# Rounding the split weights with one integer addition, and scoring two heads at once, in an attention and mixture-of-experts kernel

## The chip, the core and the metric

The program runs on one core of one Trainium2 chip. The core has TensorE (PE, matmuls and transposes), VectorE (DVE), ScalarE (ACT), GpSimd (POOL) and SyncE (SP, which here issues nearly all DMAs). Each engine executes its own queue in order and waits on semaphores for the others; a matmul writes a bank of PSUM, and every copy out of PSUM is DVE's or ACT's work. The metric is the device time of one execution, in microseconds.

## What is computed

Local attention with 32 global tokens for 4 batches of 8 heads, then a dense layer pair, then a layer in which each token goes to one of 8 experts. The arithmetic is float32; the dense weights arrive as 64-bit floats.

```python
def _attn_ref(q_l, k_l, v_l, q_g, k_g, v_g):      # (4, 8, 512 or 32, 64)
    s_g = scale * q_g @ concat(k_g, k_l).T;  out_g = softmax(s_g) @ concat(v_g, v_l)
    s_ll = scale * q_l @ k_l.T;  s_ll = where(|i - j| <= 32, s_ll, -1e9)
    s_l = concat([scale * q_l @ k_g.T, s_ll])
    out_l = softmax(s_l) @ concat(v_g, v_l)
    return concat([out_g, out_l])
def _moe_ref(x, w_in, w_out):                     # 2176 x 512, 512 x 2048, 2048 x 512
    h = x @ w_in
    return maximum(0.01 * h, h) @ w_out
def _moe2_ref(x, expert_emb, tau, w1, w2):        # 8 experts, 512 x 1024 and 1024 x 512
    logits = normalized(x) @ normalized(expert_emb).T / tau
    e = argmax(logits);  gate = softmax(logits)[e]
    return gate * (maximum(x @ w1[e], 0) @ w2[e])
```

## The kernel before

The work stands in one program order, which a scheduler turns into a queue for each engine. On PE the order is kept as written; on the other engines the scheduler chooses within the priorities given (`ahead` gives attention's parts a head start of 50).

**Attention** goes by pairs of heads, `n` = 0 to 15. `QK(n, 0)` transposes the keys and `QK(n, 1)` the queries, so that head 0 lies in partitions 0 to 63 and head 1 in 64 to 127. A unit `u` = 0 to 63 is two query blocks of 128 for one head: `S(u)` multiplies queries and keys (two matmuls of 128 rows by 224 keys), takes scores plus mask and the row minimum on DVE (line 213), the exponential with its row sum on ACT (218), adds 1e-9 and inverts the sum on DVE (222, 223), and scales block 0 on POOL and block 1 on DVE (229). For the first four head pairs the queries lie in a zero-padded tile and the matmul uses all 128 rows (line 201); later it uses the 64 rows of its head (203). The probabilities are in one of three buffers `prs`. `TR(u)` transposes them two slots later; ACT copies them out (240). `AV(p)` multiplies two units with the values, four slots after. `GS`, `GT` and `GA` do the global rows for two head pairs. `load_v` fetches the values; a second copy, shifted by 64 keys with the global values behind it (`vb`), is made by two ACT copies (116, 117).

**The dense weights** are 32 pieces of 128x512, each loaded as pairs of 32-bit words into one of two `raw` buffers. `conv_abs` takes the magnitude of the high words on ACT (357). `conv_bits` is five DVE steps: clamp (367), shift and mask (368), sign and exponent put in (371, which begins a second temporary), exponent alone (374), low word times 2^-52 times that (375). `conv_add` adds the two temporaries on POOL (384), `conv_split` rounds to the matmul's format on ACT (390) and subtracts for the remainder on POOL (391). Each `conv()` call finishes one piece, works on the next and loads ahead.

**The dense layers**: `L1(i, f)` is twelve matmuls (684) into an accumulator, then copy (ACT, 691), leaky step (DVE, 692), rounding (ACT, 694) and remainder (DVE, 695); `L2` is six matmuls (706 to 708) for two tiles of tokens, one step later. Up to slot 21 there is attention and conversion alone; then each of the first steps has one `L1`, one `L2`, one `conv()` and 0.65 slots of attention, until all pieces are converted; then the dense steps and attention go on, and the experts' layer follows (from about 660 us in the trace).

PSUM's eight banks are four pools of two, `S`, `H`, `Y` and `T`; the tables `ALONE`, `FUSED` and `MIXED` say in which pool a tile lies in each stretch (before: scores in `S`, `H`, `S`).

Of the kernel before, what the change touches and what calls it, by code (L numbers as in the profile page):

```python
# [18 lines left out]
P = 128  # L19
# [6 lines left out]
def kernel(  # L26
# [53 lines left out]
    NPAD = 4  # L80
# [24 lines left out]
    def load_v(n):  # L105
# [10 lines left out]
        nc.scalar.copy(vb[0:64], ve[0:64, 1:NC + 1])  # L116
        nc.scalar.copy(vb[64:96], ve[0:32, 0:1].to_broadcast([SG, NC, 2, D]))
# [22 lines left out]
    for t in [qz] + gzs:  # L140
        nc.vector.memset(t[D:P, 0], 0.0)
        nc.vector.memset(t[0:D, 1], 0.0)
# [7 lines left out]
    bank = {"sp": "S", "sg1": "S"}  # L150
# [6 lines left out]
    def QK(n, j):  # L157
        qn, kn, gn = natural[n]
        if j == 1:
# [4 lines left out]
            if n < NPAD:  # L164
                nc.scalar.copy(qz[0:D, 0], qv[0:D])
                nc.vector.tensor_copy(qz[D:P, 1], qv[D:P])
            else:
                nc.scalar.copy(qz[:, n % 2], qv)
# [24 lines left out]
    def S(u):  # L193
        n, c0, h = u // 4, 2 * ((u // 2) % 2), u % 2
        kT, _ = qkT[n]
        r = slice(D * h, D * h + D)
        sp = ps.tile([P, 2, WK], F32, tag=bank_of("sp"), name="sp")
        for i in range(2):
            c = c0 + i
            if n < NPAD:  # L200
                nc.tensor.matmul(sp[:, i, :], qz[:, h, c * P:(c + 1) * P], kT[:, c, :], start=True, stop=True)
            else:
# [4 lines left out]
        pr = prs[u % NPR]  # L207
        nm = att.tile([P, 2], F32, tag="nm", bufs=4, name="nm")
        sm = att.tile([P, 2], F32, tag="sm", bufs=4, name="sm")
        for i in range(2):  # L210
            c = c0 + i
            m = 0 if c == 0 else (2 if c == NC - 1 else 1)
            nc.vector.tensor_tensor_reduce(  # L213
                out=pr[:, i, 0:WK], in0=sp[:, i, :], in1=mask[:, m, :], scale=-0.125, scalar=BIG,
                op0=ALU.add, op1=ALU.min, accum_out=nm[:, i:i + 1],
            )
        for i in range(2):
            nc.scalar.activation(  # L218
                out=pr[:, i, 0:WK], in_=pr[:, i, 0:WK], func=AF.Exp, bias=nm[:, i:i + 1], scale=-1.0,
                accum_out=sm[:, i:i + 1],  # L220
# [3 lines left out]
        for i in range(2):  # L224
            eng = "pv"[i]
# [999 lines left out]
```

## Time and profile before

| | us |
|---|---|
| runs before | 965.29, 965.67, 968.04 (median 965.67) |
| the profiled execution | 967.12 |
| its span, first to last instruction | 965.4 |
| PE busy | 899.1 (93%) |
| DVE busy | 696.4 (72%) |
| ACT busy | 564.2 (58%) |
| POOL busy | 280.2 (29%) |

The profiler recorded one execution; all rows quoted come from it. Shares over the whole span mix three stages: attention with weight conversion, the dense layers with the rest of attention, and the experts. The stages have different late engines, so each is read in its own stretch. [...]

### The profile page before, as it was taken

The page shows a single profiled execution, that of the slowest core. Times are in us where ns is not written, and L with a number is a line of the kernel's source. Part 1 is how long each engine was busy: PE and PEld are TensorE (multiplying, and loading weights), DVE is VectorE, ACT ScalarE, POOL GpSimd, SP SyncE. Part 2 cuts the span into 40 slices and gives each one's busy share as a digit, 9 for nine tenths or more (in the row PEclk, how much of TensorE's full clock was granted, in tenths as well). Part 3 has the DMA queues.
Part 4 walks back from the last instruction along what each step waited for, and adds up shares of the span by engine and source line. Part 5 has one row for each costly group of instructions (what it writes and reads, how often), then busy time and mean ns, then how long its engine had stood idle before and what let it go on. Part 6 is the DMA issues. An engine that isn't in the chain of part 4 may idle for free.

```text
span 965.4 us, 16184 instructions
## 1 busy us (share of the span) xinstructions
PE 899.1 (93%) x5578; PEld 747.9 (77%) x5578; DVE 696.4 (72%) x1722; ACT 564.2 (58%) x1206; POOL 280.2 (29%) x316
## 2 busy tenths in 40 slices
PE   7688877979999999999999999997799999999997
PEld 5565766768888888887888888986687888888885
DVE  7999999997554554544553534564988999999996
ACT  6777545465545554454452323256477888888885
POOL 4767656663121121121110100020223321222211
PEclk9987988989999999999999999999799999999999
DMA  6843333341011011010000000254613416919650
GB/s 163 186 121 110 111 108 102 91 132 24 23 39 43 23 38 42 1 39 20 2 12 13 12 12 12 60 170 186 51 48 119 134 44 221 359 33 381 210 201 25
DMA packets 92454, 89.82 MB, mean 93 GB/s; under 512 B 61191, under 2 KB 69511, under 8 KB 92370
## 3 DMA queue, kind: packets, MB, share of 16 engines
q1 hardware_dynamic: 88146, 77.99, 26.6%
q0 software_dynamic: 4224, 10.78, 4.0%
q8 instruction: 45, 0.74, 0.4%
q14 instruction: 39, 0.32, 0.1%
HBM read 137.14 MB, written 11.63 MB: 154 GB/s over the span
## 4 chain that ended last, share of the span: by engine, by line
PE 62%; issue 5%; DVE 5%; DMA 3%; ACT 1%; POOL 0%; SPq 0%; POOLq 0%; DVEq 0%
PE hps L684 16%; PE hp L910 9%; PE yp L938 8%; PE yp L706 6%; PE yp L708 5%; PE yp L707 5%; PE sp L203 3%; PE av L252 2%; PE pp L238 1%; PE tp L924 1%; DVE w2s L865 1%; DVE w1s L865 1%; DMA ids<-idl 1%; PE lp L514 1%; DMA out_dram<-yo,ids 1%
## 5 line engine op out<-in xcount | busy, mean ns | idle before, releaser
L692 DVE SCALAR_TENSOR_TENSOR gf<-gf 128x256 f32<-128x256 f32 (+1 forms) x144 | 62.9, 445 | 121.0 <-ACT gf L691 120.7
L910 PE MATMUL hp<-w1s,xgT 128*128 128x512 f32 x528 | 139.0, 413 | 0.0
L691 ACT COPY gf<-hps 128x256 f32<-128x256 f32 (+1 forms) x144 | 50.1, 359 | 145.8 <-PE hps L684 143.3
L938 PE MATMUL yp<-w2s,ht 128*128 128x512 f32 x528 | 130.8, 396 | 1.0 <-DVEq L1189 1.0
L938 PEld LDWEIGHTS yp<-w2s,ht 128*128 128x128 f32 x528 | 98.8, 188 | 25.7 <-DVEq L1189 1.4
L706 PE MATMUL yp<-woh,g 128*128 128x512 f32 x272 | 115.4, 424 | 1.8 <-ACT g L694 1.8
L910 PEld LDWEIGHTS hp<-w1s,xgT 128*128 128x128 f32 x528 | 100.0, 196 | 21.2
L708 PE MATMUL yp<-woh,g 128*128 128x512 f32 x272 | 108.9, 400 | 4.3 <-DVE g L695 4.3
L229 POOL TENSOR_SCALAR pr<-pr,sm 128x224 f32<-128x224 f32 x64 | 65.4, 1021 | 160.5 <-DVE sm L223 130.3
L707 PE MATMUL yp<-wol,g 128*128 128x512 f32 x272 | 108.3, 398 | 0.0
L694 ACT CAST g<-gf 128x256 fp32r<-128x256 f32 (+1 forms) x144 | 55.3, 394 | 71.5 <-DVE gf L692 71.5
L695 DVE TENSOR_TENSOR g<-gf,g 128x256 fp32r<-128x256 f32 (+1 forms) x144 | 66.2, 468 | 31.2 <-ACT g L694 25.9
L684 PE MATMUL hps<-xs,wih 128*128 128x256 f32 x448 | 77.6, 296 | 11.0 <-DVE nm L213 11.0
L684 PEld LDWEIGHTS hps<-xs,wih 128*128 128x128 f32 x448 | 66.8, 195 | 18.4 <-DVE nm L213 12.3
L684 PE MATMUL hps<-xl,wih 128*128 128x256 f32 x448 | 72.9, 285 | 0.0
L684 PE MATMUL hps<-xs,wil 128*128 128x256 f32 x448 | 72.6, 285 | 0.0
L946 POOL DMA_INDIRECT out_dram<-yo,ids x22 | 26.2, 1191 | 157.0 <-ACT yo L945 150.2
L218 ACT ACTIVATE pr<-pr,nm 128x224 f32<-128x224 f32 x128 | 60.8, 477 | 18.2 <-DVE nm L213 17.9
L708 PEld LDWEIGHTS yp<-woh,g 128*128 128x128 f32 x272 | 51.6, 190 | 19.3 <-DVE g L695 7.1
L684 PEld LDWEIGHTS hps<-xs,wil 128*128 128x128 f32 x448 | 62.6, 194 | 0.0
L684 PEld LDWEIGHTS hps<-xl,wih 128*128 128x128 f32 x448 | 62.6, 194 | 0.0
L706 PEld LDWEIGHTS yp<-woh,g 128*128 128x128 f32 x272 | 51.4, 189 | 14.0 <-issue 4.6
(267 smaller groups left out, 1933.7 us busy)
## 6 DMA issues: line engine op xcount, KB each, us to landing
w1a<-in_moe_w_dram SPq DMA_DIRECT2D x12, 2048.0 KB
w2a<-in_moe_w_dram SPq DMA_DIRECT2D x12, 2048.0 KB
w1b<-in_moe_w_dram SPq DMA_DIRECT2D x12, 2048.0 KB
w2b<-in_moe_w_dram SPq DMA_DIRECT2D x12, 2048.0 KB
raw<-in_moe_w_in_dram SPq DMA_DIRECT2D x16, 512.0 KB
raw<-in_moe_w_out_dram SPq DMA_DIRECT2D x16, 512.0 KB
x2d<-x SPq DMA_DIRECT2D x16, 256.5 KB
kn<-in_k_l_dram SPq DMA_DIRECT2D x32, 128.0 KB
```

The lines of the kernel that those rows point to most:

```text
L218: nc.scalar.activation(out=pr[:, i, 0:WK], in_=pr[:, i, 0:WK], func=AF.Exp, bias=nm[:, i:i + 1], scale=-1.0, accum_out=sm[:, i:i + 1],)
L229: (nc.gpsimd if eng == "p" else nc.vector).tensor_scalar(out=pr[:, i, 0:WK], in0=pr[:, i, 0:WK], scalar1=sm[:, i:i + 1], scalar2=None, op0 ...
L684: nc.tensor.matmul(hps, ws[a][:, k], xs[c][k], start=(a + c + k == 0), stop=((a, c) == (1, 0) and k == KM - 1))
L691: nc.scalar.copy(gf, hps[:, cs])
L692: nc.vector.scalar_tensor_tensor(out=gf, in0=gf, scalar=0.01, in1=gf, op0=ALU.mult, op1=ALU.max)
L694: nc.scalar.copy(g[:, 0], gf)
L695: nc.vector.tensor_tensor(out=g[:, 1], in0=gf, in1=g[:, 0].bitcast(F32), op=ALU.subtract)
L706: nc.tensor.matmul(yp, g[:, 0], hi, start=(f == 0), stop=False)
L707: nc.tensor.matmul(yp, g[:, 0], lo, start=False, stop=False)
L708: nc.tensor.matmul(yp, g[:, 1], hi, start=False, stop=(f == KF - 1))
L910: nc.tensor.matmul(hp_, xT[:, a, k, :], w[:, c, k, :], start=(a + c + k == 0), stop=(c == 1 and k == KM - 1))
L938: nc.tensor.matmul(yp, ht[:, a, f, :], w[:, c, f, :], start=(j + a + c + f == 0), stop=(j == c == 1 and f == 3))
```

## The change

Three things change. **The weights**: ACT makes two passes over a raw piece, the magnitude of the high words and the low words times 2^-29 as integers; DVE does clamp, shift and mask, sign and exponent, and then one integer addition of the two, which carries the rounding into the upper bits. POOL's addition goes; all pieces now lie in one temporary from ACT's first pass to POOL's subtraction. **The scores**: one call does both heads of a query block pair, alternating between the two halves of PE's rows, into two banks; probabilities have four buffers, queries one unpadded one; the sums of two units are added to and inverted together, and the scaling is half DVE's and half ACT's instead of half POOL's. **The values**: the shifted copy is loaded by five DMAs per head pair instead of two ACT copies. The tables of banks follow.

```diff
-        nc.scalar.copy(vb[0:64], ve[0:64, 1:NC + 1])
-        nc.scalar.copy(vb[64:96], ve[0:32, 0:1].to_broadcast([SG, NC, 2, D]))
+        for h in range(2):
+            part = v_l[b, h0 + h, 96:96 + 3 * P].rearrange("(c p) d -> p c d", p=P)
+            nc.sync.dma_start(vb[0:64, 0:NC - 1, h, :], part[0:64])
+            nc.sync.dma_start(vb[64:96, :, h, :], v_g[b, h0 + h].unsqueeze(1).to_broadcast([SG, NC, D]))
+        nc.sync.dma_start(vb[0:32, NC - 1], v_l[b, hs, 480:512].rearrange("h s d -> s h d"))
...
-    NPR = 3
+    NPR = 4
-    qz = att.tile([P, 2, NC * P], F32, name="qz")
+    qz = att.tile([P, NC * P], F32, name="qz")
...
+        sps = [ps.tile([P, 2, WK], F32, tag=bank_of(f"sp{h}"), name="sp") for h in range(2)]
         for i in range(2):
             c = c0 + i
+            for h in range(2):
+                r = slice(D * h, D * h + D)
                 nc.tensor.matmul(
-                    sp[:, i, :], qz[r, n % 2, c * P:(c + 1) * P], kT[r, c, :], start=True, stop=True,
+                    sps[h][:, i, :], qz[r, c * P:(c + 1) * P], kT[r, c, :], start=True, stop=True,
                     tile_position=(D * h, 0),
                 )
...
-        for i in range(2):
-            eng = "pv"[i]
...
+        for j in range(4):
+            pr = pr2[j // 2][:, j % 2, 0:WK]
+            if j % 2:
+                nc.scalar.activation(out=pr, in_=pr, func=AF.Copy, scale=sm[:, j:j + 1])
             else:
+                nc.vector.tensor_scalar(out=pr, in0=pr, scalar1=sm[:, j:j + 1], scalar2=None, op0=ALU.mult)
...
+            nc.scalar.activation(out=pair[0].bitcast(F32), in_=raws[i][:, :, :, 1].bitcast(F32), func=AF.Abs)
+            nc.scalar.activation(out=pair[1], in_=raws[i][:, :, :, 0].bitcast(U32), func=AF.Copy, scale=2.0 ** -29)
...
-        nc.vector.tensor_scalar(out=t0, in0=t2, scalar1=-0x800000, scalar2=None, op0=ALU.bitwise_and)
-        nc.vector.scalar_tensor_tensor(
-            out=t0.bitcast(F32), in0=low.bitcast(U32), scalar=2.0 ** -52, in1=t0.bitcast(F32),
-            op0=ALU.mult, op1=ALU.mult,
-        )
-            nc.gpsimd.tensor_tensor(out=t2.bitcast(F32), in0=t2.bitcast(F32), in1=t0.bitcast(F32), op=ALU.add)
+        nc.vector.tensor_tensor(out=t, in0=t, in1=low, op=ALU.add)
...
-    ALONE = dict(sp="S", sg1="S", pp="H", av="Y", gp="Y", gq="T", ga="T", qp="T", kp="T", gnp="T")
-    FUSED = dict(sp="H", sg1="H", pp="H", av="T")
-    MIXED = dict(sp="S", sg1="S", pp="S", av="S", gp="T")
+    ALONE = dict(sp0="S", sp1="H", sg1="S", pp="Y", av="T", gp="Y", gq="T", ga="T", qp="T", kp="T", gnp="T")
+    FUSED = dict(sp0="H", sp1="T", sg1="H", pp="H", av="T")
+    MIXED = dict(sp0="S", sp1="T", sg1="S", pp="S", av="S", gp="T")
```

How the queues move is seen at three places. In the changed kernel's order the names are the same and the line numbers differ by a few.

On ACT, around the first copy of a dense accumulator (`gf<-hps`), before: `t` is a first pass over a raw piece, `wih` and `woh` the rounding, `pr` an exponential.

```order
L390 CAST woh<-t_989 128x512
L357 ACTIVATE t_1094<-raw 128x512
L218 ACTIVATE pr_99,sm<-pr_99,nm 128x224 x2
L261 COPY xr<-av 128x256
L240 COPY pT<-pp 128x512
L282 ACTIVATE pg,gm<-sg_1136,gm 128x512
L283 ACTIVATE pg,gm<-sg_1137,gm 128x32
L691 COPY gf<-hps 128x256
```

And now, where L359 and L360 are the two passes, L382 the rounding, L217 the exponentials and L226 the scalings:

```order
L382 CAST wih<-t_1221 128x4x128
L217 ACTIVATE pr_97,sm<-pr_97,nm 128x224 x2
L217 ACTIVATE pr_98,sm<-pr_98,nm 128x224 x2
L360 ACTIVATE t_1349<-raw 128x512
L259 COPY xr<-av 128x256
L238 COPY pT<-pp 128x512
L359 ACTIVATE t_1348<-raw 128x512
L382 CAST woh<-t_1278 128x512
L226 ACTIVATE pr_97<-pr_97,sm 128x224
L226 ACTIVATE pr_98<-pr_98,sm 128x224
L682 COPY gf<-hps 128x256
```

Exponentials of two units stand together and their scalings in the same queue behind them. Ahead of this first copy stand 10 passes over raw pieces and 8 roundings before, 30 and 14 now; 12 copies of values before, none now; 22 scalings now.

On DVE, one piece of the conversion among attention's work, before:

```order
L374 TENSOR_SCALAR t_872<-t_989 128x512
L223 RECIPROCAL sm<-sm 128x2
L213 ISA pr_98,nm<-sp,mask 128x224
L213 ISA nm 128x1
L213 ISA pr_98,nm<-sp,mask 128x224
L213 ISA nm 128x1
L375 SCALAR_TENSOR_TENSOR t_872<-raw,t_872 128x512
L229 TENSOR_SCALAR pr_99<-pr_99,sm 128x224
```

And now, from the third step (L372) and the integer addition (L375) on:

```order
L372 SCALAR_TENSOR_TENSOR t_1278<-raw,t_1278 128x512
L375 ISA t_1278<-t_1278,t_1279 128x1024
L221 TENSOR_SCALAR sm<-sm 128x4
L222 RECIPROCAL sm<-sm 128x4
L228 TENSOR_SCALAR pr_97<-pr_97,sm 128x224
L228 TENSOR_SCALAR pr_98<-pr_98,sm 128x224
L368 TENSOR_SCALAR t_1348<-t_1348 128x512
```

The addition is a special instruction that the order lists over 1024 elements, two 16-bit halves of each of the 512 words; the sums of two units (128x4) go through one add and one reciprocal.

On PE, one step of the dense layers with scores and AV in it, after the conversion has ended, before:

```order
L684 MATMUL hps<-xs,wil 128x256 x4
L203 MATMUL sp<-kT,qz 128x224 x2
L252 MATMUL av<-pT,ve_110 64x128 x2
L252 MATMUL av<-pT,vb_112 64x128 x2
L252 MATMUL av<-pT,ve_110 64x128 x2
L252 MATMUL av<-pT,vb_112 64x128 x2
L706 MATMUL yp<-woh,g 128x512
```

And now:

```order
L675 MATMUL hps<-xs,wil 128x256 x4
L200 MATMUL sp<-kT,qz 128x224 x4
L250 MATMUL av<-pT,ve_109 64x128 x2
L250 MATMUL av<-pT,vb_111 64x128 x2
L250 MATMUL av<-pT,ve_109 64x128 x2
L250 MATMUL av<-pT,vb_111 64x128 x2
L697 MATMUL yp<-woh,g 128x512
```

The four score matmuls of two units stand together where AV stands, and the odd slot that held two of them before holds none.

## Rows read from the trace of the kernel before

**Rows 1.** Busy us by stretch: PE, PEld, DVE, ACT, POOL; clock; DMA share; GB/s.

```profile
0.00:86.00 86.00, 66.49 (x502) 49.10 (x503) 77.13 (x275) 62.18 (x171) 53.26 (x83) 0.90 0.61 148
86.00:225.00 139.00, 114.38 (x764) 93.24 (x762) 136.30 (x292) 74.15 (x187) 86.77 (x75) 0.91 0.37 106
225.00:660.00 435.00, 432.31 (x2960) 373.50 (x2959) 217.08 (x838) 196.11 (x561) 67.48 (x95) 1.00 0.13 37
0.00:10.00 10.00, 4.55 (x15) 3.54 (x16) 5.17 (x25) 3.68 (x5) 4.28 (x27) 1.00 0.61 139
```

**Rows 2.** Groups of DVE, 0 to 225: count, busy us, mean ns, idle.

```profile
L375 DVE SCALAR_TENSOR_TENSOR t<-raw,t 128x512 f32<-128x512 uint32 x32 | 29.1, 911 | 0.3
...
L222 DVE TENSOR_SCALAR sm<-sm 128x2 f32<-128x2 f32 x35 | 12.2, 347 | 1.0 <-ACT pr L218 0.8
```

**Rows 3.** Lines of DVE, 0 to 225: shortest/median/longest ns, first, last start.

```profile
L375 DVE SCALAR_TENSOR_TENSOR t<-raw,t x32: 670/687/1785, 23.7 to 224.7; 128x512 f32<-128x512 uint32 x32
...
L374 DVE TENSOR_SCALAR t<-t x32: 403/416/1515, 22.8 to 224.2; 128x512 int32<-128x512 int32 x32
...
L222 DVE TENSOR_SCALAR sm<-sm x35: 146/161/1255, 11.4 to 224.1; 128x2 f32<-128x2 f32 x35
```

**Rows 4.** Timeline at 162: start us, us, engine, instruction.

```profile
161.72 1.71 POOL L391 TENSOR_TENSOR wil<-t,wih 128x512 fp32r<-128x512 f32 x1 [1.65 <-ACT wih L390]
...
162.23 1.48 DVE L695 TENSOR_TENSOR g<-gf,g 128x256 fp32r<-128x256 f32 x1
```

**Rows 5.** Groups of POOL, 0 to 225.

```profile
L384 POOL TENSOR_TENSOR t<-t,t 128x512 f32<-128x512 f32 x31 | 43.4, 1400 | 23.2 <-DVE t L375 17.6 <-DVE sm L222 4.0 <-DVE gm L287 1.0
...
L391 POOL TENSOR_TENSOR wil<-t,wih 128x512 fp32r<-128x512 f32 x16 | 22.5, 1406 | 13.1 <-ACT wih L390 13.1
```

**Rows 6.** Groups of ACT, 0 to 225.

```profile
L218 ACT ACTIVATE pr<-pr,nm 128x224 f32<-128x224 f32 x70 | 33.3, 477 | 16.7 <-DVE nm L213 16.6
...
L357 ACT ACTIVATE t<-raw 128x512 f32<-128x512 f32 x32 | 21.7, 677 | 9.3 <-DMA raw<-in_moe_w_out_dram 5.4 <-DMA raw<-in_moe_w_in_dram 3.8
...
L390 ACT CAST wih<-t 128x512 fp32r<-128x512 f32 x16 | 9.9, 617 | 2.9 <-POOL t L384 2.9
...
L694 ACT CAST g<-gf 128x256 fp32r<-128x256 f32 x21 | 8.5, 407 | 32.1 <-DVE gf L692 32.1
...
L117 ACT COPY vb<-ve 32x512 f32<-32x512 f32 x10 | 6.2, 617 | 1.1 <-DMA ve<-in_v_g_dram 0.6
```

**Rows 7.** Timeline of SP at 14: issue of the first raw piece.

```profile
14.32 0.43 SPq L345 DMA_DIRECT2D raw<-in_moe_w_in_dram  x1
```

**Rows 8.** Timeline of PE, 300 to 311, where it is always busy.

```profile
300.50 1.02 PE L203 MATMUL sp<-kT,qz 64*128 64x224 f32 x4
...
301.45 0.66 PE L238 MATMUL pp<-ident,pr 128*128 128x128 f32 x4
...
301.87 0.48 PE L706 MATMUL yp<-woh,g 128*128 128x512 f32 x1
...
303.35 0.63 PE L684 MATMUL hps<-xs,wih 128*128 128x256 f32 x4
...
304.77 0.60 PE L178 MATMUL kp<-ident,kn 128*128 128x128 f32 x4
...
309.46 0.44 PE L252 MATMUL av<-pT,ve 128*64 128x128 f32 x4
...
310.48 0.50 PE L706 MATMUL yp<-woh,g 128*128 128x512 f32 x1
```

**Rows 9.** Group of PE, 225 to 660: the scores.

```profile
L203 PE MATMUL sp<-kT,qz 64*128 64x224 f32 x116 | 29.6, 375 | 0.0
```

**Rows 10.** Timeline of ACT and POOL: first pass and subtraction of piece 16.

```profile
125.75 0.67 ACT L357 ACTIVATE t<-raw 128x512 f32<-128x512 f32 x1 [1.21 <-DMA raw<-in_moe_w_in_dram]
...
139.18 1.29 POOL L391 TENSOR_TENSOR wil<-t,wih 128x512 fp32r<-128x512 f32 x1
```

**Rows 11.** Single line of ACT: all first passes.

```profile
L357 ACT ACTIVATE t<-raw x32: 651/674/700, 19.0 to 217.0; 128x512 f32<-128x512 f32 x32
```

More of the change, by code (lines that the diff above doesn't have):

```diff
@@ L149 @@
     qkT, units, groups = {}, {}, {}
-    bank = {"sp": "S", "sg1": "S"}
+    bank = {"sp0": "S", "sp1": "H", "sg1": "S"}
     def bank_of(name):
@@ L163, in QK @@
             qv = qp.rearrange("k c p -> k (c p)")
[L164 to L168, printed above, removed]
+            nc.scalar.copy(qz, qv)
             natural.pop(n)
@@ L217, in S @@
-        for i in range(2):
+        pr2 = [prs[(2 * p + h) % NPR] for h in range(2)]
+        nm = att.tile([P, 4], F32, tag="nm", bufs=2, name="nm")
+        sm = att.tile([P, 4], F32, tag="sm", bufs=2, name="sm")
+        for h in range(2):
+            for i in range(2):
+                c, j = c0 + i, 2 * h + i
+                m = 0 if c == 0 else (2 if c == NC - 1 else 1)
+                nc.vector.tensor_tensor_reduce(
+                    out=pr2[h][:, i, 0:WK], in0=sps[h][:, i, :], in1=mask[:, m, :], scale=-0.125, scalar=BIG,
+                    op0=ALU.add, op1=ALU.min, accum_out=nm[:, j:j + 1],
+                )
@@ L223, in S @@
         nc.vector.reciprocal(out=sm, in_=sm)
-        for i in range(2):
-            eng = "pv"[i]
-            if eng == "a":
-                nc.scalar.activation(out=pr[:, i, 0:WK], in_=pr[:, i, 0:WK], func=AF.Copy, scale=sm[:, i:i + 1])
-            else:
-                (nc.gpsimd if eng == "p" else nc.vector).tensor_scalar(
-                    out=pr[:, i, 0:WK], in0=pr[:, i, 0:WK], scalar1=sm[:, i:i + 1], scalar2=None, op0=ALU.mult
-                )
-        units[u] = pr
+        for j in range(4):
+            pr = pr2[j // 2][:, j % 2, 0:WK]
+            if j % 2:
+                nc.scalar.activation(out=pr, in_=pr, func=AF.Copy, scale=sm[:, j:j + 1])
+            else:
+                nc.vector.tensor_scalar(out=pr, in0=pr, scalar1=sm[:, j:j + 1], scalar2=None, op0=ALU.mult)
+        for h in range(2):
+            units[2 * p + h] = pr2[h]
     def TR(u):
@@ L351, in conv_load, with conv_round @@
             raws[i] = t
-    def conv_abs(i):
+    def conv_round(i):
         if wide and i in raws:
-            t0 = sb.tile([P, DM], I32, tag="x2T", bufs=2, name="t0")
-            t0 = temps[i] = t0.rearrange("p (k n) -> p k n", k=raws[i].shape[1])
-            nc.scalar.activation(out=t0.bitcast(F32), in_=raws[i][:, :, :, 1].bitcast(F32), func=AF.Abs)
+            pair = []
+            for k in range(2):
+                t = sb.tile([P, DM], I32, tag=("x2T", "x2")[k], bufs=2, name=f"t{k}")
+                pair.append(t.rearrange("p (k n) -> p k n", k=raws[i].shape[1]))
+            temps[i] = pair
+            nc.scalar.activation(out=pair[0].bitcast(F32), in_=raws[i][:, :, :, 1].bitcast(F32), func=AF.Abs)
+            nc.scalar.activation(out=pair[1], in_=raws[i][:, :, :, 0].bitcast(U32), func=AF.Copy, scale=2.0 ** -29)
     def conv_bits(i):
@@ L388, in conv_split @@
             hi, lo = conv_dst(i)
-            src = temps.pop(i)[1].bitcast(F32) if wide else raws.pop(i)
+            src = temps.pop(i).bitcast(F32) if wide else raws.pop(i)
             nc.scalar.copy(hi, src)
@@ L979, in att_parts @@
             parts.append(lambda: GS(m))
-        if n < NU:
-            parts.append(lambda: ahead(50, S, n))
+        if n < NU and n % 2 == 0:
+            parts.append(lambda: ahead(50, S, n // 2))
         if 1 == 1 and n % 4 == 3 and m + 1 < NHP:
```

48 lines of the change are left out of this document (14 added, 34 removed).

## The prediction

> **What bounds the kernel now.** I read the busy time by stage first [rows 1]. VectorE (DVE) is busy 77.1 of the first 86 us and 136.3 of the next 139, 213.4 of 225 in all; TensorE (PE) has gaps there and part of that time its slow clock (granted 0.90 and 0.91). From 225 to 660 PE is busy 432.3 of 435 at full clock. The change touches nothing behind 660. So there are two accounts: to 225 the question is what is late once DVE is lighter, and from 225 to 660 only what leaves PE counts.
>
> Then the groups of DVE instructions to 225 [rows 2] beside the shortest of the same instructions [rows 3]. The last conversion step, on line 375, takes 911 ns in the mean and its shortest is 670; the tiny add on line 222 takes 347 and its shortest 146. Mean minus shortest, times the count, summed over nine groups (375, 371, 367, 374, 368, 229, 695, 692 and 222) is 64 us: DVE is not computing in it, it is held. The timeline names the holder [rows 4]: GpSimd's (POOL's) two-input subtraction runs 161.72 to 163.43, and a DVE subtraction of 128x256 that starts at 162.23 takes 1.48 us and ends 0.28 us after it.
>
> **DVE to 225, part by part.** (a) POOL's conversion add on line 384 goes (43.4 us of two-input work); its subtraction on line 391 stays (32 pieces at about 1.4 us, alike) [rows 5]. By those shares half of the 64 us of holding goes: -32. Ends: 0, if the remaining subtraction finds other victims, and -64. POOL's scaling on line 229 goes too; it has one tensor input and I count no more for it.
> (b) Of five DVE steps per piece two leave, 374 and 375, at their shortest 403 + 670 ns [rows 3]; the holding is in (a). An integer add comes. The order shows it as a special instruction over 128x1024, that is over 16-bit halves. No such row exists. From below, a two-input step over 128x512 words is 670 ns; from above, if each half takes as long as a word, it is twice that, 1.34 us. I take 680, because the bytes moved are those of the first. 32 x (0.68 - 1.07) = -12.5; at the upper end +9.
> (c) The add and reciprocal on the sums now serve two units: half of 35 x 2 x 146 ns, with the reciprocal counted like the add, is -5. Four DVE copies of queries go, 512 wide like a step of 670: -3.
> 213.4 - 32 - 12.5 - 5 - 3 = 161 of 225: DVE no longer sets this stage.
>
> [...]
>
> **ScalarE (ACT) is late next.** It gains a second pass over each raw piece, strided like the one on line 357, at 677 ns, and half of the probabilities' scalings: 128x224, for which the nearest row is the cast of 128x256 at 407. It loses the copies into the shifted values, 617 (line 117; those on line 116 I count alike) [rows 6]. In its queue, ahead of the first copy of the dense layer's accumulator, now stand 30 passes over raw pieces where there were 10, 14 casts where there were 8 (617), 22 scalings more, 2 exponentials more, 12 value copies fewer: 13.5 + 3.7 + 9.0 + 1 - 7.4 = +19.8. ACT was busy 62.2 before 86 us and idle 6.3 of the first 10 [rows 1]. 62.2 + 19.8 + 6.3 = 88 us if it never waits again. It will: its scalings wait for DVE's reciprocal, and everything else of ACT, the exponentials of the next pair among it, is queued behind them. The ten DMAs more of the first two value loads stand ahead of the first raw piece on SP, 0.43 us or more each [rows 7], so that piece comes 4 to 5 us later; ACT has attention work meanwhile. I take 10% of waiting after the first 10 us: the first copy comes at 97 us, where it is 86 now. Ends: 90 and 110. So **the attention-only stretch gets longer**; it has six more pieces converted at its end.
>
> **PE from there to its bound stretch.** Its order is fixed; the work up to what now is reached at 225 is 22 steps of the dense layers and 15 units of attention. Prices, from the stretch at full clock [rows 8]: six second-layer matmuls 301.87 to 303.35, 1.48; twelve first-layer ones to 304.77, 1.42; four transposes 301.45 to 301.87, 0.42; eight AV matmuls 309.46 to 310.48, 1.02; one unit of scores 300.50 to 301.45, 0.95. 22 x 2.9 = 64. A pair of units is scores (1.16, below) + 0.84 + 1.02 = 3.0, and 7.5 pairs are 23. Key and query transposes and the global rows I put at 9. Sum 96, where the stretch takes 139 now. Of their 156 and 161 us ACT and DVE have by rough shares 70 and 80 left for it, so PE leads. [...] With 3% of waits: 97 + 99 = 196, against 225: **-29**. Ends: 90 + 96 = 186, and 110 + 110 = 220.
>
> **PE from 225 to 660.** 116 records on line 203 are 29 units, that is 14.5 pairs [rows 9]. Two units apart cost 1.90. Together they lie between 0.95 (halves fully at once) and 1.90 (not at all). The nearest row is AV, whose two column halves alternate: 16 records in 1.02 are 64 ns each, while the transposes, same columns on the full array, take 105. 1.90 x 64/105 = 1.16; 14.5 x 0.74 = **-10.7**, ends 0 and -13.8. What else happens there is at no price: ACT's extra scalings find it at 196 of 435 busy, and the next accumulator is not ready before the transposes and two dense groups behind the scores have run, some 3.8 us against about 3.5 for the pair's softmax. If that cover is gone, each pair costs PE a few tenths, 5 us at most. The second bank comes from the pool of the short transposes.
>
> [...]
>
> **Sum.** Against the profiled execution (967.12, span 965.4): -29 - 10.7 = 927.4. That execution lies 1.45 above the median of the runs, 965.67, which leaves **926**.
>
> **Rivals.** *The waits of the one queue eat the stage.* ACT waits for DVE, DVE for ACT, four exponentials in a row; stretch one 110, stretch two 115, so nothing is won before 225 and only the scores' 10.7 remain: 955. For it: ACT already waits 16.6 us for DVE's minima on line 218 at lower load [rows 6], and both engines are at some 160 of 196. Against: DVE's 32 us of holding are real time.
> *The halves don't overlap.* Then a pair is 1.90 there as well and stretch two 5 us longer: 942.
> *More is won:* hardly any waits, stage end at 186, scores 13.8: 913.
> *Slower: the ring of buffers.* Each piece now lives in one of two buffers from ACT's first pass to the end of POOL's subtraction; before, one buffer ended at POOL's add and another began in mid-chain. In the trace a piece takes from 125.75 to 139.18 + 1.29 = 140.5, 14.7 us [rows 10]. The pace now is 12.8 us per two pieces (32 first passes from 19.0 to 217.0) [rows 11]. If the way stays at 14.7, it sets the pace, the last piece is 15.5 x 1.9 = 29 us late, and PE waits for its weights: 965.7 + 29 - 11 = 984. From 12.8 on it costs. Against: the add (1.4 and its wait) and one DVE step leave the way, which alone makes about 12, and DVE's holding halves.
> *The change does nothing here:* DVE's time is refilled and halves don't overlap, 963 to 968.
>
> **How the numbers follow.** Forecast (912 to 940) 0.58; weak (940 to 961) 0.19; halves not overlapped 0.09; more won 0.05; nothing 0.03; ring 0.06. Range: down to 910 and up to 957, which leaves out part of "more", the end of "weak", "nothing" and "ring". A measurement here can tell about 0.3% from no change, 2.9 us. Faster 0.91 (the first four), same 0.03, slower 0.06.
>
> **What would show it.** Right: to about 195 us ACT and DVE at 80 to 90% each, POOL near 30%; the medians of lines 367 and 222's successors close to their shortest; the integer add near 0.68; the first copy of an accumulator after 90 us; PE near full from about 97 on and without gaps from 200; a pair of scores in 1.0 to 1.2. Wrong: the add at 1.3, DVE steps still held; a pair at 1.9; ACT idle for tens of us behind scalings that wait for reciprocals, or first passes that wait for POOL.

## The result and the profile after

The changed kernel takes 939.75 us (median of 4 runs, 938.37 to 940.23) against 965.91 (4 runs) for the kernel before on the same chip: ratio 0.9727, 95% interval 0.9708 to 0.9746. That is 26.2 us faster. The forecast was 926, with a range of 910 to 957. The sign held, and so did the relief of DVE and the overlap of the halves; the waiting in the first stretch did not come out as I had it. The size came out a third short, as the sum of two errors of opposite sign.

The profiled execution took 938.37 us (span 936.7). Its engines over the whole span:

```profile
PE 869.3 (93%) x5578; PEld 731.6 (78%) x5578; DVE 640.6 (68%) x1623; ACT 586.4 (63%) x1270; POOL 169.2 (18%) x220
```

The same stretches as in [rows 1], after the change (columns as there: PE, PEld, DVE, ACT, POOL, clock, DMA share, GB/s):

```profile
0.00:86.00 86.00, 56.57 (x422) 43.75 (x423) 61.37 (x219) 62.15 (x170) 23.15 (x54) 0.80 0.64 161
86.00:225.00 139.00, 120.89 (x907) 101.06 (x908) 109.61 (x293) 98.34 (x250) 36.98 (x38) 0.93 0.42 113
225.00:660.00 435.00, 427.38 (x3003) 372.44 (x3003) 221.30 (x833) 207.64 (x581) 39.42 (x65) 0.98 0.17 46
```

DVE has gone from 77.1 to 61.4 and from 136.3 to 109.6. It is no longer full, yet neither is ACT (62.2 and 98.3), and the first 86 us have less PE work in them than before, at a clock of 0.80 instead of 0.90. Stretches of equal length no longer hold equal work, so the comparison needs a mark in the work. The dense steps are one: their order on PE is the same in both kernels, and each step begins with the first of twelve weight loads. The table reads their starts from the traces, one profiled execution each; they lie about 0.1 us above the timeline's figures, alike in every row. Step 24 is where PE has stopped waiting in both kernels; after step 86 no attention is left. The kernel before, timed beside each run, took 965.9 to 967.1 us, so wholes of different runs compare to about 1 us.

| kernel | whole, median us | step 0 starts | step 22 | step 24 | steps 24 to 86 take |
|---|---|---|---|---|---|
| before | 965.9 | 85.5 | 223.4 | 231.8 | 277.6 |
| changed | 939.75 | 97.8 | 214.6 | 221.2 | 259.2 |
| e1, values copied | 941.42 | 98.7 | 209.1 | 215.7 | 269.2 |
| e2, raw early | 940.54 | 107.2 | 214.1 | 220.7 | 259.2 |
| e3, weights alone | 948.40 | 87.4 | 208.3 | 215.9 | 275.7 |
| e4, scores alone | 963.09 | 106.8 | 231.2 | 237.7 | 267.5 |
| e5, AV in Y | 942.87 | 105.5 | 220.6 | 227.1 | 259.2 |
| e6, units first | 934.98 | 104.9 | 215.0 | 221.5 | 259.1 |
| e7, values mixed | 931.38 | 96.2 | 206.5 | 213.0 | 259.2 |
| e8, heads in turn | 940.69 | 99.8 | 216.9 | 223.4 | 259.7 |
| e9, before, unpadded | 975.85 | 92.3 | 233.3 | 240.9 | 275.9 |
| e10, padded units first | 928.03 | 95.5 | 205.1 | 211.7 | 259.0 |
| e11, four raw buffers, other weights | 967.84 | 106.0 | 216.0 | 222.6 | 259.2 |
| e12, earlier dense | 924.34 | 81.7 | 198.5 | 207.7 | 260.3 |

The first account gave 10.6 us (step 24), not 29; the second gave 18.4, not 10.7. From step 86 to the end nothing changes. (That is the profiled pair, 28.7 us apart in span; the medians are 26.2 apart.) In e12 the marks at steps 22 and 24 have less attention behind them than in the other rows; its section says by how much.

### The profile page after: what moved, and what is told of

The parts are those of the page before. It is cut to its first block, busy times and chain, and to the rows that moved or that the text cites. A ratio compares the mean times of both kernels' runs of the same rounds, so it can differ in the third digit from the quotient of the medians.

```text
span 936.7 us, 16036 instructions
## 1 busy us (share of the span) xinstructions
PE 869.3 (93%) x5578; PEld 731.6 (78%) x5578; DVE 640.6 (68%) x1623; ACT 586.4 (63%) x1270; POOL 169.2 (18%) x220
## 3 DMA queue, kind: packets, MB, share of 16 engines
q1 hardware_dynamic: 100690, 80.87, 28.7%
## 4 chain that ended last, share of the span: by engine, by line
PE 69%; DVE 12%; DMA 7%; issue 6%; ACT 4%; SPq 1%; POOL 0%; POOLq 0%; DVEq 0%; ACTq 0%
PE hps L675 19%; PE hp L901 9%; PE yp L929 8%; PE yp L697 7%; PE yp L699 6%; PE yp L698 6%; DMA raw<-in_moe_w_in_dram 3%; PE sp L200 2%; PE pp L236 2%; PE av L250 2%; DVE t L372 2%; DMA raw<-in_moe_w_out_dram 2%; PE tp L915 1%; DVE w2s L856 1%; DVE w1s L856 1%
## 5 line engine op out<-in xcount | busy, mean ns | idle before, releaser
L683 DVE SCALAR_TENSOR_TENSOR gf<-gf 128x256 f32<-128x256 f32 (+1 forms) x144 | 60.4, 427 | 125.0 <-ACT gf L682 124.8
L901 PEld LDWEIGHTS hp<-w1s,xgT 128*128 128x128 f32 x528 | 99.8, 196 | 21.3
L686 DVE TENSOR_TENSOR g<-gf,g 128x256 fp32r<-128x256 f32 (+1 forms) x144 | 60.7, 430 | 38.9 <-ACT g L685 34.2
L217 ACT ACTIVATE pr<-pr,nm 128x224 f32<-128x224 f32 x128 | 60.4, 475 | 6.2 <-DVE nm L211 5.3
L856 DVE TENSOR_TENSOR w2s<-w2a,w2s 128x1024 fp32r<-128x1024 f32 x48 | 56.6, 1219 | 2.9 <-ACT w2s L855 2.9
L856 DVE TENSOR_TENSOR w1s<-w1a,w1s 128x1024 fp32r<-128x1024 f32 x48 | 56.6, 1218 | 2.0 <-ACT w1s L855 1.9
```

The costliest lines, as they stand in the source:

```text
L217: nc.scalar.activation(out=pr, in_=pr, func=AF.Exp, bias=nm[:, j:j + 1], scale=-1.0, accum_out=sm[:, j:j + 1],)
L683: nc.vector.scalar_tensor_tensor(out=gf, in0=gf, scalar=0.01, in1=gf, op0=ALU.mult, op1=ALU.max)
L686: nc.vector.tensor_tensor(out=g[:, 1], in0=gf, in1=g[:, 0].bitcast(F32), op=ALU.subtract)
L856: nc.vector.tensor_tensor(out=w[:, 1, c], in0=src[:, c], in1=w[:, 0, c].bitcast(F32), op=ALU.subtract)
L901: nc.tensor.matmul(hp_, xT[:, a, k, :], w[:, c, k, :], start=(a + c + k == 0), stop=(c == 1 and k == KM - 1))
```

## Where the second account comes from

In the changed kernel, full PE, one dense step with its attention (timeline of PE; start, us, engine, instruction):

```profile
208.03 1.03 PE L200 MATMUL sp<-kT,qz 64*128 64x224 f32 x8
208.99 0.44 PE L250 MATMUL av<-pT,ve 128*64 128x128 f32 x4
```

From its start to the next start a pair of score units takes 208.99 - 208.03 = 0.96 us (its record of 1.03 us reaches past that), where one unit took 0.95 [rows 8]. Summing the distance from each score weight load to the next one on PE over steps 24 to 86, 14 pairs take 13.4 us instead of 26.5. The same sum shows 3.8 us less for the first dense layer and 1.7 less for the query transposes. One event of the kernel before is part of that: at 449 us PE waits 1.8 us for a rounding on ACT that stands behind a value copy, and the granted clock from 448 to 460 is 0.86. What made the rest wasn't traced.

The halves overlap fully: the first two score matmuls start 7 ns apart, and a pair takes 0.96 us, not my 1.16.

**e8** asks whether this needs the alternating order.

```diff
-        for i in range(2):
-            c = c0 + i
-            for h in range(2):
+        for h in range(2):
+            for i in range(2):
+                c = c0 + i
```

> The changed kernel with the four score matmuls of a pair in the order head 0 block 0, head 0 block 1, head 1 block 0, head 1 block 1, so that neighbours lie mostly on the same half of PE's rows; banks, sums and scalings unchanged. Overlap theory (halves run at once only when neighbours alternate): a pair takes 1.4 to 1.9 us of full PE instead of 0.96, 14 pairs cost 6 to 13 us more and the whole is 945 to 953. Rival (the saving comes from issuing the pair as one run of matmuls, and from the single queries buffer): a pair stays within 0.95 to 1.1 and the whole within 2 us of 939.8.

It takes 940.69 us and a pair still takes 310.74 - 309.77 = 0.97. The overlap theory in my form, that neighbours must alternate, is wrong:

```profile
309.77 1.03 PE L200 MATMUL sp<-kT,qz 64*128 64x224 f32 x8
310.74 0.50 PE L697 MATMUL yp<-woh,g 128*128 128x512 f32 x1
```

The records behind that row start in twos, 13 ns apart, where records of one half alone start 189 ns apart (line 203 of the kernel before, median at a granted clock of 1.00). They do not name the head; since one half's own records start 189 ns apart, I take the second of each two for head 1's, although both matmuls of head 0 stand ahead of it in PE's queue. What was needed is the two halves' work next to each other, not its inner order.

## Where the first account went: the two halves of the change

**e3** puts the new rounding of the weights alone into the kernel before (`conv_round`, the three DVE steps and the integer addition). **e4** is the other half: the changed kernel with the old rounding, and with the values copied by ACT.

```diff
-        conv_add(i)
-        conv_abs(i + 1)
+        conv_round(i + 1)
```

> The kernel before with only the new rounding of the weights (two ACT passes, three DVE steps, integer addition, no addition on POOL); scores, probabilities, values and banks as before. If the 64 us of holding on DVE and the two long DVE steps were what set the stage, its part of the gain shows here: step 22 of the dense layers starts at 205 to 212 us (223.4 before, 214.6 changed), nothing changes behind it, and the whole is 952 to 958. If the holding only moved to the remaining POOL work (its scaling of probabilities stays here), step 22 starts at 216 to 222 and the whole is 960 to 966.

```diff
-        conv_round(i + 1)
+        conv_add(i)
+        conv_abs(i + 1)
```

> The changed kernel with the old rounding of the weights (POOL's addition and five DVE steps back) and the shifted values copied by ACT: the scores' part alone. If DVE's conversion steps set the first stage, step 22 stays at 220 to 228 us and only the steps behind gain: 14 pairs of scores at 0.96 instead of 1.92 us and the query transposes and waits that went with them, 15 to 19 us; the whole is 946 to 954. If PE's score time set the first stage too, step 22 comes at 208 to 216 and the whole is 936 to 942.

The weights alone give 948.40, ratio 0.981 (0.9786 to 0.9833): 15.9 us at step 24. The scores alone give 963.09, ratio 0.9967 (0.9948 to 0.9985): they lose 5.9 us by step 24 and win 10.1 behind it. So the first expectation held at step 22 (208.3) and was exceeded in the whole, 3.6 us under its 952 to 958; the second failed: I had not thought that the scores' part costs anything early.

The weight terms themselves stand as forecast. After the change, DVE's groups to 215 us (columns as [rows 2]) and the spread of single lines (as [rows 3], but over the whole run):

```profile
L372 DVE SCALAR_TENSOR_TENSOR t<-raw,t 128x512 int32<-128x512 int32 x32 | 29.5, 923 | 0.4
L375 DVE CUSTOM_DVE_ANT_0 t<-t,t 128x1024 uint16<-128x1024 uint16 x32 | 24.9, 779 | 0.3
```

```profile
L375 DVE CUSTOM_DVE_ANT_0 t<-t,t x32: 670/684/1653, 31.7 to 189.9; 128x1024 uint16<-128x1024 uint16 x32
...
L368 DVE TENSOR_SCALAR t<-t x32: 404/422/1518, 27.5 to 186.3; 128x512 f32<-128x512 f32 x32
...
L221 DVE TENSOR_SCALAR sm<-sm x32: 150/170/516, 12.3 to 448.2; 128x4 f32<-128x4 f32 x32
```

The integer addition takes 684 ns in the median, where I took 680. The clamp's median (L368) is 422 near its shortest 404; it was 569. Mean minus shortest times the count, over the eight groups that remain, is 29.6 us where it was 64: the holding has halved.

## Is it the loads of weights?

In the changed kernel ACT waits for raw pieces (waits of ACT, 0 to 215: us in total, times, longest):

```profile
ACT t L360 <- DMA raw<-in_moe_w_in_dram: 7.7, 6, 2.1
...
ACT t L360 <- DMA raw<-in_moe_w_out_dram: 6.2, 6, 3.1
...
ACT t L359 <- DMA raw<-in_moe_w_in_dram: 4.5, 3, 3.3
```

And the first piece is issued at 22.10 instead of 14.32 [rows 7], 7.8 us later where I had 4 to 5, behind ten value loads (timeline of SP):

```profile
21.63 0.43 SPq L119 DMA_DIRECT2D vb<-in_v_l_dram  x1
22.10 0.43 SPq L343 DMA_DIRECT2D raw<-in_moe_w_in_dram  x1
```

**e2** moves the first two raw loads ahead of the third pair's keys and queries and the second value load; **e11** gives the raw pieces four buffers.

```diff
     load_v(0)
     load_qk(1)
+    for i in range(2):
+        conv_load(i)
     load_qk(2)
     load_v(1)
-    for i in range(2):
-        conv_load(i)
```

> The changed kernel with the first two raw pieces loaded ahead of the second pair's queries and values on SP; nothing else differs. Loads theory: the first raw load is issued near 12 us, conversion starts about 9 us earlier, and the first dense step starts 3 to 8 us earlier than 97.8; the whole is 3 to 6 us shorter. Queue theory: conversion runs ahead of need anyway, the first dense step stays within 2 us of 97.8 and the whole within 2 us of 938.4.

```diff
-            t = att.tile([P, 2 * DM], I32, tag="raw", bufs=2, name="raw")
+            t = att.tile([P, DM], I32, tag="raw", bufs=4, name="raw")
...
-        if i + 2 < NCV:
-            conv_load(i + 2)
+        if i + 4 < NCV:
+            conv_load(i + 4)
```

> The changed kernel with raw pieces of half the size in four buffers, loaded four pieces ahead. It leaves out the reading of the dense weights: the words come from half-sized pieces of the experts' weights, each used twice, so the numbers are others while every instruction of the conversion stays. Ring theory (each of the two raw buffers is always either loading, 3.4 us, or waited for, so that conversion goes at 5.2 us per piece, and ACT's queue stands behind passes that wait 18 us in all for their loads): those waits vanish, conversion ends at 165 to 180 us instead of 192.7, and step 24 starts 4 to 12 us before 221.2. Rival (conversion runs ahead of need; PE waits for other things): conversion ends earlier but step 24 stays within 3 us of 221.2.

Neither moves step 24 by more than 1.4 us, and step 0 comes later in both, at 107.2 (outside both of e2's ranges) and 106.0. With four buffers ACT's waits on raw pieces shrink to one (waits of ACT in e11, same stretch):

```profile
ACT t L363 <- DMA raw<-in_moe_w_dram: 3.4, 1, 3.4
```

and the last piece's subtraction starts at 179.8 instead of 191.3; PE gains nothing from it. (Its whole time can't be compared: the part behind step 86 takes 484 us instead of 456, presumably because other weights send the tokens to other experts.) So the raw loads, their ring and their size together, decide the pace of conversion, but conversion is ahead of need. The prediction's slower rival, the ring of two temporaries, would show as first passes on ACT that wait for POOL's subtraction: in the changed kernel they do so once, for 0.2 us. In e11 they do so 8 times, for 5.9 us: the ring of temporaries is what comes next.

## The value loads: a cost early, a gain late

**e1** takes back the value loads.

```diff
-        for h in range(2):
-            part = v_l[b, h0 + h, 96:96 + 3 * P].rearrange("(c p) d -> p c d", p=P)
-            nc.sync.dma_start(vb[0:64, 0:NC - 1, h, :], part[0:64])
...
+        nc.scalar.copy(vb[0:64], ve[0:64, 1:NC + 1])
+        nc.scalar.copy(vb[64:96], ve[0:32, 0:1].to_broadcast([SG, NC, 2, D]))
```

> The changed kernel with the shifted values made by two ACT copies per head pair again, as before the change, instead of five loads. Loads theory (the extra loads on SP and in the transfer queues make keys and raw weight pieces late, which is why the first dense step starts at 97.8 us instead of 85.5): the first raw load is issued near 15 us instead of 22.1, the first dense step starts at 90 to 93, and the whole is 4 to 8 us shorter than 938.4. Queue theory (ACT and DVE waiting for each other set the first stretch, loads are hidden): ACT carries 7 us more before the first dense step, which starts at 98 to 104, and the whole is 0 to 6 us longer.

The first raw load is back at 14.37, but step 0 stays at 98.7 and the whole hardly moves, 941.42: by these two marks the queue theory held and the loads seem hidden. The later steps show two effects of some size that nearly cancel: step 24 comes 5.5 us sooner, and the steps behind it take 10.0 us longer. The reason for the second stands in e1's waits from 230 to 490, first of all engines, then of PE:

```profile
ACT vb L116 <- DMA ve<-in_v_g_dram: 15.1, 3, 9.0
```

```profile
PE yp L694 <- ACT g L682: 5.1, 3, 3.4
...
PE av L247 <- ACT pT L235: 2.4, 1, 2.4
```

A value copy stands at the head of ACT's queue until its load has landed, up to 9.0 us, and what stands behind it, the rounding of a dense step's result or a copy of transposed probabilities, keeps PE waiting: 7.5 of the 10.0 us. In the changed kernel no copy is there. I had given the value loads no price behind 225; with pairs of scores they are worth some 10 us there. Without them the second account would have been 8.4 us, less than the 10.7 forecast. Of the whole little shows that, because the cost to step 24 (5.5 us) hides half of the gain: two prices that I had left out nearly cancel, which is luck.

**e7** makes use of both: copies for the early pairs, loads for the late ones.

```diff
+        if n < 8:
+            nc.scalar.copy(vb[0:64], ve[0:64, 1:NC + 1])
+            nc.scalar.copy(vb[64:96], ve[0:32, 0:1].to_broadcast([SG, NC, 2, D]))
+        else:
...
```

> The changed kernel with the shifted values copied by ACT for head pairs 0 to 7 and loaded for 8 to 15. From the run with all copies (step 24 at 215.7 instead of 221.2, but 10 us less gained from there to step 86, with PE waiting for roundings on ACT that stand behind copies which wait up to 9 us for value loads) the loads cost in the first stage and pay in the second: step 24 at 214 to 218, the later gain 16 to 19 us, the whole 932 to 936. If the copies of pairs 0 to 7 are the ones that hold ACT late, or the loads in the second stage are slow in themselves, the whole is 938 to 943.

931.38 us (ratio 0.965, 0.9606 to 0.9694). Step 24 comes at 213.0, 8.2 us sooner than in the changed kernel, and the later steps keep their 259.2. Step 24 and the whole lie a little past the expected ranges. The profiled execution, 928.65, is the fastest of four that reach to 934.16, so the 8.2 may be some us too large. In the changed kernel PE waits for keys in the first 98 us, and for a bank that an AV accumulator holds; with copies the wait for the loads of keys is gone. PE's waits, changed kernel and then e7:

```profile
PE gnp L181 <- ACT xr L259: 7.8, 3, 3.9
PE kp L176 <- DMA kn<-in_k_l_dram: 7.1, 2, 4.1
```

```profile
PE gnp L185 <- ACT xr L263: 5.5, 4, 2.3
...
PE kp L180 <- POOL tok L441: 3.9, 1, 3.9
```

Whether it is SP's issuing (five more issues per pair, some 3 us: from 6.49 to 9.67 for the first) or the transfers that make the keys late wasn't separated. That e2 wins nothing by putting raw pieces first, and keys later, agrees with either. Nor are the value loads the only thing that makes keys late: e3, which copies the values, waits 4.2 us for them.

## The bank, the pairing, and the clock

The wait for the bank suggested that AV should go back to pool Y. **e5** does that, one word in `ALONE`.

```diff
-    ALONE = dict(sp0="S", sp1="H", sg1="S", pp="Y", av="T", gp="Y",
+    ALONE = dict(sp0="S", sp1="H", sg1="S", pp="Y", av="Y", gp="Y",
```

> The changed kernel with one word of the table ALONE put back: AV's accumulator lies in pool Y again (beside the transposed probabilities) instead of T, where the transposes of keys, queries and globals lie. Banks theory (in the attention-only stretch the small transposes of the globals wait 7.8 us on PE for ACT to copy an AV accumulator out of T): that wait goes, the first dense step starts at 90 to 94 us instead of 97.8, step 24 at 214 to 219 instead of 221.2, and the whole is 932 to 937. Queue theory (the pair's chain over DVE and ACT sets the stretch, and the bank only shows where PE waits): the wait comes back at another instruction, the first dense step stays at 96 to 100 and the whole within 3 us of 939.8.

It is no faster: 942.87, where the kernel before beside it took 967.06, and step 24 comes 5.9 us later. The wait has moved, and grown (PE's waits in e5, 0 to 105):

```profile
PE pp L236 <- ACT xr L259: 12.0, 3, 6.1
```

A pair's scores now hold two banks at once, and in either pool that was tried for AV something waits for a bank; by step 24 the table that came with the change is the better one of the two.

**e6** goes back to single units, old banks and old scaling for the first 22 units, with pairs only from there (`S1` is the old `S` for one unit, on the 64 rows of its head).

```diff
-        if n < NU and n % 2 == 0:
+        if n < SLOT0 + 1:
+            parts.append(lambda: ahead(50, S1, n))
+        elif n < NU and n % 2 == 0:
             parts.append(lambda: ahead(50, S, n // 2))
```

> The changed kernel, but in the attention-only stretch (22 units) scores go by single units in the old order and banks, with the old split of the scaling between POOL and DVE; pairs begin with the dense steps. If pairing is what lengthens that stretch, the first dense step starts at 85 to 90 us (85.5 before, 87.4 with the new rounding alone, 97.8 changed), step 24 at 214 to 218, and with the later gain kept the whole is 930 to 935. If the value loads lengthen it, the first dense step stays at 95 to 99 and the whole at 937 to 942.

In the profiled execution step 0 doesn't come back, 104.9, and step 24 is where it was. But that execution, 937.32, is one of the slower two of four (930.87 to 938.50), and the median, 934.98, lies at the edge of the pairing theory's 930 to 935. So e6 doesn't settle whether pairing lengthens the first stretch. Its single units also run on 64 rows, and its windows show something else:

```profile
60.00:80.00 20.00, 20.00 (x139) 14.51 (x131) 15.37 (x55) 14.21 (x39) 9.80 (x13) 0.63 0.47 138
```

PE is busy all the time, at a granted clock of 0.63. What e6 does not take back is the padding: the kernel before ran the first four pairs' scores over all 128 rows, half of them zero. **e9** takes only that from the kernel before.

```diff
-    NPAD = 4
+    NPAD = 0
```

> The kernel before with one number changed: the zero-padded queries of the first four head pairs (matmuls over all 128 rows) become plain ones over the 64 rows of their head, as the change does too. Clock theory (in the run with single units first, PE was busy 20.0 of 20 us from 60 to 80 at a granted clock of 0.63, against 1.00 from 20 to 60 in the kernel before; what differs on PE there is that only half of its rows work in the scores): the clock between 20 and 60 us falls from 1.00 to 0.6 to 0.8, the first dense step starts at 90 to 97 us instead of 85.5, and step 24 of the dense layers is 4 to 12 us late. Rival (padding is only another way to pick a head, and the clock follows PE's gaps): the clock stays at 0.95 to 1.00 up to 60 us, two DVE copies per pair are saved, and the first dense step starts at 83 to 87.

975.85 us, ratio 1.0111 (1.0066 to 1.0156): slower by 8.8. The first dense step starts at 92.3. The windows of before, then of e9:

```profile
40.00:60.00 20.00, 14.55 (x120) 10.71 (x120) 19.71 (x68) 15.71 (x47) 14.77 (x18) 1.00 0.74 150
60.00:80.00 20.00, 16.77 (x129) 12.00 (x133) 18.61 (x59) 16.03 (x42) 12.07 (x13) 0.74 0.49 125
```

```profile
40.00:60.00 20.00, 18.86 (x115) 13.41 (x113) 17.12 (x59) 14.53 (x39) 11.67 (x12) 0.69 0.62 146
60.00:80.00 20.00, 17.86 (x114) 13.61 (x114) 19.73 (x57) 13.35 (x38) 15.74 (x15) 0.57 0.38 99
```

With these scores on half of the rows the granted clock is 0.69 instead of 1.00 and 0.57 instead of 0.74 (from 20 to 40 it is still 0.97), PE is busier with fewer instructions, and step 24 is 9.1 us late, though DVE is spared a copy of queries per pair. The scores themselves cost the same: in the kernel before, at a granted clock of 1.00, one score weight load follows the other after 189 ns in the median when padded (line 201) and 188 when not (line 203). This is a part of the change that I had booked as a gain of 3 us. e3, which is padded too, had 0.71 from 40 to 60, so the two windows here are not the rule for every padded kernel.

**e10** puts padded single units for the first four pairs into e7 (the fourth buffer of probabilities begins where the padded half ends). One part of the computation is changed in it: the first new pair overwrites the probabilities of unit 15 before they are read; every instruction runs.

```diff
-        if n < NU and n % 2 == 0:
+        if n < 4 * NPAD:
+            parts.append(lambda: ahead(50, S1, n))
+        elif n < NU and n % 2 == 0:
```

> The run with values copied for pairs 0 to 7, and the first four head pairs as in the kernel before: padded queries, single units, three buffers of probabilities, the old banks, half the scaling on POOL; from pair 4 on pairs of heads as changed (the fourth buffer of probabilities takes the place of the padded half). Clock theory: clock 0.9 to 1.0 between 20 and 60 us, the first dense step at 84 to 90 us instead of 96.2, step 24 at 202 to 209 instead of 213.0, whole 920 to 927. Rival (the first stretch is set by ACT's and DVE's work and the loads, not by PE's clock): the first dense step at 93 to 99, step 24 at 211 to 217, whole 929 to 936.

928.03 us (ratio 0.9603, 0.9582 to 0.9624), step 24 at 211.7: only 1.3 us better than e7 (3.4 by the medians). The clock theory's numbers failed here, for the first dense step (95.5), step 24 and the whole; the rival's held for the two steps. The windows of e7, then of e10:

```profile
20.00:40.00 20.00, 14.47 (x116) 11.32 (x116) 15.14 (x53) 16.48 (x47) 7.21 (x10) 0.70 0.83 186
40.00:60.00 20.00, 12.21 (x85) 8.79 (x81) 19.39 (x53) 17.59 (x43) 5.96 (x7) 0.70 0.62 172
```

```profile
20.00:40.00 20.00, 12.97 (x126) 10.38 (x125) 14.32 (x50) 15.36 (x43) 9.50 (x13) 1.00 0.76 170
40.00:60.00 20.00, 14.94 (x95) 10.87 (x96) 18.67 (x67) 16.01 (x47) 9.17 (x11) 0.74 0.55 150
60.00:100.00 40.00, 24.38 (x224) 18.00 (x221) 37.80 (x113) 36.11 (x95) 18.48 (x20) 0.91 0.53 144
```

The clock came back from 20 to 40, but from 60 to 100 DVE and ACT are busy 37.8 and 36.1 of 40, and PE 24.4. A reading that fits, though no run isolates it: where those two set the pace PE's clock costs little (1.3 us at step 24 between e7 and e10), and in e9, where PE was busy 17.9 to 18.9 of 20, it costs much (9.1 us at step 24).

## One queue, and when the dense steps begin

What they are busy with at that point can be read off the changed kernel. Its first copy of a dense accumulator, which I forecast for 97, starts at 105.5, while the matmuls ended near 99.3 (timeline, rows of DVE, ACT, POOL and PE):

```profile
98.70 0.62 PE L675 MATMUL hps<-xs,wil 128*128 128x256 f32 x4
...
98.90 0.66 ACT L359 ACTIVATE t<-raw 128x512 f32<-128x512 f32 x1 [0.66 <-DMA raw<-in_moe_w_out_dram]
...
100.53 0.48 ACT L217 ACTIVATE pr<-pr,nm 128x224 f32<-128x224 f32 x1
...
102.13 1.54 POOL L286 TENSOR_TENSOR pg<-pg,gm 128x544 f32<-128x544 f32 x1
...
102.40 0.65 ACT L360 ACTIVATE t<-raw 128x512 int32<-128x512 uint32 x1
...
102.86 1.36 DVE L375 CUSTOM_DVE_ANT_0 t<-t,t 128x1024 uint16<-128x1024 uint16 x1
102.95 0.35 ACT L259 COPY xr<-av 128x256 f32<-128x256 f32 x1
103.21 0.57 ACT L238 COPY pT<-pp 128x512 f32<-128x512 f32 x1
103.69 0.67 ACT L359 ACTIVATE t<-raw 128x512 f32<-128x512 f32 x1
104.14 0.16 DVE L221 TENSOR_SCALAR sm<-sm 128x4 f32<-128x4 f32 x1
104.26 0.61 ACT L382 CAST woh<-t 128x512 fp32r<-128x512 f32 x1
104.33 0.18 DVE L222 RECIPROCAL sm<-sm 128x4 f32<-128x4 f32 x1
...
104.78 0.85 ACT L226 ACTIVATE pr<-pr,sm 128x224 f32<-128x224 f32 x2
...
105.53 0.35 ACT L682 COPY gf<-hps 128x256 f32<-128x256 f32 x1
...
105.93 1.23 PE L675 MATMUL hps<-xs,wih 128*128 128x256 f32 x4 [4.97 <-ACT gf L682]
```

Read from the end: PE waits 4.97 us for the copy; the copy stands on ACT behind two scalings, a cast, a pass, two copies, another pass, and four exponentials, and from 98.90 on none of them shows a wait: ACT is busy all the way to the copy. DVE is late too (its integer addition takes 1.36 us beside POOL's multiplication of global probabilities), but the reciprocal ends at 104.51, before the cast ahead of the scalings does (104.87), so ACT doesn't wait for it. It is the order of the one queue that costs here, and not ACT's waiting for DVE, which the rival had. Counting PE's distances from one weight load to the next that exceed the mean of the same instruction in steps 24 to 86 by more than 0.4 us, the changed kernel has 14 such gaps in steps 0 to 24, 20.0 us in all, and the kernel before 21 with 31.9.

PE's order has nothing else to offer in the attention-only stretch. **e12** gives it something: the arrangement of e10, with the buffers renumbered so that no unit is overwritten, and two slots of attention fewer ahead of the first dense step.

```diff
-    SLOT0 = 21
+    SLOT0 = 19
```

> The previous arrangement (values copied for pairs 0 to 7, padded single units for pairs 0 to 3, pairs of heads from 4 on; with the buffers of probabilities renumbered so that no unit is overwritten before it is read), and the dense steps begin after 19 slots of attention instead of 21. Order theory (PE's gaps in the attention-only stretch, some 50 of 95 us, are there because nothing else is in its order): the first dense step starts at 84 to 91 us instead of 95.5, step 24 at 204 to 209 instead of 211.7, whole 921 to 926. Rival (ACT and DVE, 37 of 40 us busy from 60 to 100, set the stage by their work, and PE's gaps only move): the first dense steps start earlier, but step 24 stays within 2 us of 211.7 and the whole at 926 to 930.

924.34 us, ratio 0.9561 (0.9541 to 0.9582), the fastest here: 15.4 us under the changed kernel, 3.7 under e10. Step 24 comes at 207.7, 4.0 sooner than in e10, but with less attention done: PE has 1349 weight loads behind it instead of 1362 (at step 22 it is 1278 instead of 1318). At step 28 both have 1438, and e12 is 2.7 us ahead. Step 0 comes at 81.7, even before the order theory's 84 to 91; its ranges for step 24 and the whole held, so PE's gaps were partly a matter of when the dense steps were put in; a part of the gain at step 24 is work that only comes later.

## Point by point

- **DVE to 225, 161 forecast.** Right. It is 168 us, up to 215 (with ACT's 157); the halved holding, the addition at 0.68 and the shared sums are as sized. POOL's one-input scaling, to which I gave no share of the holding, shows none: in the kernel before, line 375's step takes 680 ns in the median beside no work of POOL (13 times), 681 beside the scaling alone (6) and 1461 beside two-input work (13).
- **The first accumulator copy at 97 (90 to 110).** It came at 105.5. ACT's work ahead of it was as counted (62.2 + 19.8 = 82 forecast), but not its waiting:

```profile
0.00:106.00 106.00, 67.96 (x521) 51.77 (x521) 79.05 (x273) 79.38 (x217) 30.50 (x62) 0.81 0.62 160
```

79.4 busy, 26.6 idle, where I had 6.3 and 10% of the rest. The failing step is this 10%, and [rows 1] already spoke against it: before, ACT was idle 23.8 of the first 86 us, 17.5 of them after the first 10. My 88 us and these 17.5 make 105.8, the right size, though the waits need not be the same ones. Now they are not those that I named, for reciprocals (1.0 us up to 215, none ahead of the copy), but mainly these (waits of ACT, 0 to 105.6):

```profile
ACT pr L217 <- DVE nm L211: 5.0, 4, 2.5
ACT kT L177 <- PE kp L176: 4.7, 2, 3.1
ACT t L359 <- DMA raw<-in_moe_w_in_dram: 4.4, 2, 3.3
ACT t L360 <- DMA raw<-in_moe_w_out_dram: 3.8, 2, 3.1
ACT t L360 <- DMA raw<-in_moe_w_in_dram: 2.4, 2, 1.9
```

The value loads explain only a part: without them (e1, e7) ACT is idle 16.5 and 14.2 us ahead of the copy, but busy 87.8, and the copy comes at 104.3 and 102.0. With one wait for a raw piece left in the first 215 us (e11) it comes at 110.4. What sets the rest of the 8.5 us is open.
- **Stretch two, 99 us with 3% of waits.** From the copy to step 22 it took 109.1. The price of the work was right: by each instruction's mean distance at full PE, steps 0 to 24 need 100.5 us and took 123.4, most of the rest (20.0) in 14 long gaps. The failing step is the 3%.
- **Together: step 22 at 196 forecast, 214.6 measured.** Of these 18.6 us, the value loads account for 8.1 (e7), padded units for 1.4 (e10), and the late start of the dense steps for 2.7 (e12, at step 28, where its work is the same). The last 6.4 are not settled, and each figure is from single executions, which scatter by a few us (e7's runs span 928.65 to 934.16).
- **The scores, -10.7 (0 to -13.8).** -13.1: AV's row was the wrong neighbour, the lower end nearly right. The 5 us beside them were not forecast, nor that the value loads keep ACT's queue free there: with copies (e1) only 8.4 of the 18.4 are won.
- **Rivals.** "The one queue" took a part of the stage, not all of it, and by the order of ACT's queue and its waits for loads and minima, not by scalings that wait for reciprocals. "Halves don't overlap" and "the ring of buffers" are refuted, by the pair at 0.96 and by the 0.2 us of waiting for POOL.

## What to carry to other kernels

Cost a load that replaces a copy twice, for what it makes late and for the wait that it takes out of the copying engine's queue; here the answer changed sign at step 24 (5.5 us lost up to it, 10.0 won behind it). When the late engine is relieved, look at the order of the others before counting their busy time: the next bound was neither ACT nor DVE by load (79.4 and 79.1 busy of the first 106 us), but where work stood in their queues. And compare stages at a mark in the work, not by the whole: e1 looked like nothing and was two effects of 5 and 10 us.

## What the runs showed of the hardware

Matmuls on the two row halves run side by side even when two of one head stand ahead of the other's (e8: starts 13 ns apart, 0.97 us for a pair; alternating: 7 ns and 0.96), against 0.95 us for one unit. With the first four pairs' scores on 64 rows instead of 128 padded ones (e9) the granted clock from 40 to 60 us was 0.69 instead of 1.00, and the kernel before lost 8.8 us; padded kernels with other work around the scores had 0.71 (e3) and 0.74 (e10) there. An integer addition of 512 words, done as 1024 halves of 16 bits, takes 684 ns on DVE, as much as a two-input step over the words (693 on line 372).
